# Attention and SoLU feed-forward on one core: q and k loaded in rows of eight tokens, and both turned by TensorE

## Chip, cores and metric

The kernel runs on one core of a Trainium2 chip. The metric is the device time of one execution in microseconds, from several executions; a time named "span" is the length of one profiled execution as the trace has it.

## What is computed

Four sequences of 768 tokens, eight heads of 64, go through an attention with a local window of 96 keys and eight global keys. The result, one row of 512 per token, goes through a feed-forward layer with the SoLU activation and a norm.

```python
batch, n_heads, seq, head_dim = (4, 8, 768, 64); n_global, n_local = (8, 96)
scores = scale * np.matmul(q, k.transpose(0, 1, 3, 2))
keep = is_global | is_local
scores = np.where(keep, scores + bias[None], -1e9)      # bias: -slope(head) * distance
a = softmax(scores); attn_out = np.matmul(a, v)
x = attn_out.transpose(0, 2, 1, 3).reshape(B * S, H * D)
h = x @ w_in                                            # 512 -> 1024
solu = h * softmax(h)
ln = (solu - mean) / sqrt(var + 1e-6) * g_ln
out = ln @ w_out                                        # 1024 -> 512, 3072 rows, float32
```

Inputs and output are float32; the kernel multiplies in fp16.

## The kernel before

**Units.** The work is cut into twelve units of 256 tokens (`UQ`), unit u being the stretch u mod 3 of sequence u div 3. A unit needs its own q, k and v (512 KB each) and, except the first of a sequence, the last keys of the unit before.

**Steps.** Every piece of work is a step with a short name, and the string `ORDER` (line 25) is the whole program: line 640 runs its steps in that order, each engine and each DMA queue gets its instructions in that order, and nothing is rearranged later. A letter after a step's name is the engine or queue (S SyncE, A ScalarE, P GpSimd, D VectorE), numbers are the unit and the head pair, half or token tile. The steps that matter here:

- `q`, `k`, `v` (lines 147 and 155): loads into a staging pool of 13 buffers (line 145). For q and k, a partition takes two neighbouring tokens of each of the eight heads, so a run in HBM is 512 bytes. v goes in two halves of 128 tokens, in runs of 256 bytes.
- `cq`, `ck`, `cv` (287, 291): casts to fp16, on any of three engines.
- `tk` and `tq` (295): eight 128x128 transposes on TensorE into one of two PSUM buffers with the tag "small" (line 128). `ek` (310) evacuates k and puts its tokens in order with a strided read; `eq` (306) evacuates q as it stands. Units 0, 1 and 2 turn q this way. The other nine units turn q with `dq` (315), a transpose done by the DMA queue from SBUF to SBUF.
- q therefore stays in an order of even tokens, then odd tokens, and so do the masks (`off`, 173), the scores `S` (328), the sums `L` (388), the weighted values `V` (418) and the normed result `N` (442). The store (551) writes rows "(p r)", two neighbouring tokens per partition, which this order fits.
- `X` (341) is the exponential of a head pair's scores on ScalarE, `M` (347) the multiplication with the mask on VectorE, `mask` (281) the sixteen mask tables on ScalarE, `I` (412) the reciprocal of the sums on ScalarE as two activations, `gk`, `gS`, `gX`, `gv0`, `gv` the eight global keys.
- The feed-forward of a token tile of 128: `A` (454, eight matmuls of 512 columns), `E` (468, exp on ScalarE), `U` (476, product on VectorE), `Q` (486, squares on ScalarE), `Z` (492, the norm's factors on GpSimd), `d` (527, DMA transpose of the product), `O` (531, eight matmuls of 512 columns), `o` (540, scaling out of PSUM), `st` (551, store).
- `wi` (559) loads w_in from GpSimd's queue with a cast; `warm` (226) issues matmuls on zeros whose result nobody reads.

PSUM: three double-bank buffers with the tag "big" (line 125), shared by `S`, `L`, `V` and `A`; two "small" ones, shared by turned tiles, `gS`, `gv`, `O` and `warm`. A step that asks for a buffer waits until the tile two (small) or three (big) allocations back has been read.

Of the kernel before, what the change touches and what calls it, by code (L numbers as in the profile page):

```python
# [18 lines left out]
UQ = 256  # L19
FAR = 30000.0  # L20
# [17 lines left out]
cq:P:5 k:S:5 ck:P:5 mean S:4:0 X:4:0 S:4:3 X:4:3 ce:0 ce:1 cq:D:6 ce:2 ce:3 ce:4 cm sm:5 sm:6 pr:7
v:S:6:0 q:S:7 A:2:0 gv:1 M:3:0 A:1:0 Q:0:0 E:2:0 U:2:0 Z:P:0:0 gk:2 E:1:0 U:1:0 A:1:1 v:S:4:0
E:1:1 U:1:1 L:3 I:3 tk:5 ek:D:5 sm:7 V:3 gS:4 Q:1:0 A:2:1 E:2:1 dq:S:5 N:3 S:5:0 X:5:0 M:4:3 A:3:0  # L40
E:3:0 S:5:3 gX:4 X:5:3 S:5:1 X:5:1 d:S:0:1 O:0:1 k:S:7 dq:S:6 d:S:0:0 S:5:2 X:5:2 gS:5 v:S:4:1
v:S:6:1 S:6:0 gX:5 X:6:0 U:2:1 Q:2:1 U:3:0 cq:D:7 dq:S:7 A:3:1 E:3:1 ck:D:7 S:6:3 cv:P:6 X:6:3
q:S:8 v:S:5:0 v:S:5:1 M:4:1 M:4:2 M:4:0 cv:P:4 gv0:2 Z:P:1:0 L:4 I:4 tk:7 O:0:0 S:6:1 X:6:1
o:A:0:0 M:5:0 o:D:0:1 cq:P:8 M:5:3 M:5:1 cv:P:5 U:3:1 M:5:2 ek:D:7 V:4 N:4 S:6:2 X:6:2 k:S:8 S:7:0
X:7:0 gv:2 gS:6 gX:6 v:S:7:0 v:S:7:1 S:7:1 X:7:1 S:7:3 X:7:3 L:5 I:5 M:6:3 M:6:0 V:5 N:5 A:4:0
E:4:0 ck:P:8 tk:8 ek:D:8 Q:2:0 Z:P:2:1 Z:P:2:0 Q:1:1 S:7:2 X:7:2 M:7:1 M:7:3 A:5:0 E:5:0 dq:S:8
U:4:0 d:S:1:0 O:1:0 d:S:2:0 M:6:2 o:D:1:0 U:5:0 k:S:9 d:S:1:1 S:8:2 X:8:2 Q:3:0 S:8:0 X:8:0
Z:P:1:1 ck:P:9 q:S:9 q:S:10 M:7:0 O:2:0 o:D:2:0 M:7:2 M:6:1 k:S:10 tk:9 S:8:1 X:8:1 ek:D:9 gk:3
cv:P:7 ck:P:10 A:4:1 E:4:1 L:6 U:4:1 k:S:11 d:S:2:1 cq:D:10 dq:S:10 I:6 S:8:3 X:8:3 d:S:3:1 O:1:1
o:D:1:1 d:S:3:0 V:6 cq:D:9 dq:S:9 Q:3:1 v:S:8:0 st:S:0 gS:8 gS:7 gX:7 v:S:8:1 v:S:9:0 v:S:9:1  # L50
d:S:4:0 A:5:1 d:S:5:0 gX:8 N:6 tk:10 Q:4:0 E:5:1 L:7 I:7 Z:P:3:1 Q:5:0 ck:D:11 A:6:0 tk:11 q:S:11
st:S:1 ek:D:10 M:8:1 U:5:1 d:S:5:1 d:S:4:1 M:8:0 ek:D:11 M:8:2 V:7 N:7 Q:4:1 S:10:0 E:6:0 gS:10
gX:10 X:10:0 O:2:1 o:A:2:1 O:3:1 U:6:0 M:8:3 Q:6:0 Z:P:3:0 Q:5:1 cv:P:8 S:10:3 S:9:3 X:9:3 M:9:3
X:10:3 Z:P:4:0 Z:P:5:1 st:S:2 A:6:1 E:6:1 U:6:1 Q:6:1 v:S:10:0 v:S:10:1 O:3:0 o:D:3:0 o:D:3:1
A:7:0 E:7:0 U:7:0 A:7:1 E:7:1 U:7:1 M:10:3 Z:P:5:0 cq:P:11 dq:S:11 O:4:0 o:D:4:0 Q:7:0 S:10:2
X:10:2 Q:7:1 V:8 L:8 I:8 N:8 M:10:0 S:10:1 cv:A:9 X:10:1 O:5:0 o:A:5:0 O:5:1 o:A:5:1 d:S:6:0
st:S:3 Z:P:7:0 Z:P:4:1 gv0:3 M:10:2 A:8:0 E:8:0 U:8:0 M:10:1 A:8:1 gv:3 E:8:1 U:8:1 O:4:1 S:11:1
X:11:1 Z:P:6:0 L:10 I:10 S:9:2 S:11:2 Z:P:6:1 Z:P:7:1 cv:P:10 o:D:4:1 X:11:2 O:6:0 X:9:2 d:S:6:1
O:6:1 d:S:8:0 st:S:5 S:9:1 X:9:1 st:S:4 S:9:0 X:9:0 Q:8:0 o:D:6:0 M:9:2 o:D:6:1 gS:9 M:9:0 d:S:7:1
v:S:11:0 d:S:7:0 Z:P:8:0 V:10 N:10 M:9:1 gX:9 S:11:3 S:11:0 X:11:0 O:8:0 X:11:3 M:11:1 gS:11 gX:11  # L60
L:9 o:A:8:0 I:9 V:9 N:9 st:S:6 d:S:8:1 M:11:0 A:10:0 E:10:0 Q:8:1 v:S:11:1 U:10:0 M:11:3 M:11:2
cv:P:11 A:10:1 E:10:1 A:9:0 U:10:1 E:9:0 U:9:0 Q:10:1 O:7:0 o:A:7:0 Q:9:0 L:11 I:11 V:11 N:11
Z:P:8:1 Q:10:0 A:9:1 Z:P:9:0 d:S:10:0 E:9:1 U:9:1 Z:P:10:1 O:7:1 o:A:7:1 A:11:0:0 d:S:9:0 O:8:1
o:A:8:1 Z:P:10:0 A:11:0:1 A:11:1:0 E:11:0:0 Q:9:1 O:10:0 E:11:0:1 o:A:10:0 U:11:0:0 E:11:1:0
Q:11:0:0 O:9:0 d:S:9:1 U:11:0:1 U:11:1:0 A:11:1:1 E:11:1:1 U:11:1:1 st:S:8 o:A:9:0 Z:P:9:1 O:9:1
o:A:9:1 d:S:10:1 O:10:1 o:A:10:1 Q:11:0:1 t:11:0:0 e:D:11:0:0 t:11:0:1 e:D:11:0:1 st:S:7 t:11:1:0
e:D:11:1:0 t:11:1:1 e:A:11:1:1 O:11:0:0 O:11:0:1 st:S:10 O:11:1:0 O:11:1:1 st:S:9 Z:P:11:0:1
o:D:11:0:0 o:D:11:0:1 st:S:11:0:1 Q:11:1:0 Q:11:1:1 Z:P:11:1:1 o:A:11:1:1 o:D:11:1:0 st:S:11:0:0
st:S:11:1:0 st:A:11:1:1
# [4 lines left out]
def kernel(  # L74
# [23 lines left out]
    QC = UQ // 2  # L98
    assert NL % 2 == 0 and NL < P and NG % 2 == 0 and 2 * NG <= 32 and H == 8
# [47 lines left out]
    def load_qk(queue, name, u):  # L147
        b, s = units[u]
        t = held[name + "32", u] = staged([P, H, 2 * D], name + "32")
        queues[queue].dma_start(  # L150
            out=t,
            in_=(q if name == "q" else k)[b, :, ts(s, UQ)].rearrange("h (p r) d -> p h (r d)", r=2),
        )
# [19 lines left out]
    def offsets(kind):  # L173

        w = (W0, W1)[kind]
        qi = held["qi", kind] = msb.tile([P, w], I32, name=f"qi{kind}", tag="osb", bufs=3)
        for j, a, e, o in blocks(kind)[0]:
            n = (e - a) // 2
            nc.gpsimd.iota(
                qi[:, o : o + 2 * n].rearrange("p (r i) -> p r i", r=2),  # L180
                pattern=[[1, 2], [2, n]], base=kind * UQ + a - j * P, channel_multiplier=-1,
            )
# [43 lines left out]
    def warm_up(n):  # L226

        t = small([P, 512], FP32, "warm")
        for _ in range(n):
            nc.tensor.matmul(out=t, lhsT=held["zeros"][:, 0:P], rhs=held["zeros"],  # L230
                             start=True, stop=True)
# [55 lines left out]
    def cast_qk(engine, name, u):  # L287
        t = held[name + "16", u] = attn.tile([P, 2, H, D], FP16, name=name + "16")
        cast(engine, t, held.pop((name + "32", u)).rearrange("p h (r d) -> p r h d", r=2))
# [5 lines left out]
    def turn(name, u):  # L295
        src = held.pop((name + "16", u))
        t = held["p" + name, u] = small([P, 2, NPAIR, P], FP16, name + "turned")
        for r in range(2):
            for g in range(NPAIR):
                nc.tensor.transpose(  # L300
                    out=t[:, r, g, :],
                    in_=src[:, r, 2 * g : 2 * g + 2].rearrange("p h d -> p (h d)"),
                    identity=held["ident"],
                )

    def evac_q(engine, u):
        t = held["qT", u] = attn.tile([P, 2, NPAIR, QC], FP16, name="qT")
        cast(engine, t, held.pop(("pq", u)))

    def evac_k(engine, u):  # L310
        t = held["kT", u] = attn.tile([P, NPAIR, UQ], FP16, name="kT", bufs=4)
        cast(engine, t.rearrange("p g (i r) -> p g i r", r=2),
             held.pop(("pk", u)).rearrange("p r g i -> p g i r"))

    def turn_q_dma(queue, u):
        t = held["qT", u] = attn.tile([P, 2, NPAIR, QC], FP16, name="qT")
        queues[queue].dma_start_transpose(
            out=t.rearrange("p r g i -> p (r g) i"),
            in_=held.pop(("q16", u)).rearrange("p r h d -> p (r h d)"),
        )  # L320
# [7 lines left out]
    def scores(u, g):  # L328
# [3 lines left out]
        for j, a, e, o in blocks(s)[0]:  # L332
            for m in range(2):
                r = slice(m * D, m * D + D)
                nc.tensor.matmul(  # L335
                    out=sc[:, m, o : o + e - a].rearrange("p (r i) -> p r i", r=2),
                    lhsT=held["kT", u - s + j // 2][r, g, ts(j % 2, P)],
                    rhs=qT[r, :, g, a // 2 : e // 2], start=True, stop=True,
                )
# [14 lines left out]
    def gstart(s):  # L354
        return 0 if s else G0 // 2

    def global_scores(u):
# [3 lines left out]
        n = QC - i0  # L361
        gs = held["gs", u] = small([P, 2, n], FP32, "gs")
# [314 lines left out]
```

## Time and profile before

| | |
|---|---|
| median of 5 executions | 182.15 us (181.33 to 185.22) |
| the profiled execution | 180.99 us, its span 179.3 us |
| mean TensorE clock granted | 0.965 |
| busy in the span: TensorE, ScalarE, VectorE, GpSimd | 149.3, 144.2, 113.1, 86.4 us |
| DMA: share of the 16 engines on SyncE's and ScalarE's loads and stores (queue q1) | 89.0% |
| q and k: 12 loads each of 512 KB, median time from issue to landing | 6.7 and 7.0 us |
| DMA transposes: 9 of q, 22 in the feed-forward | 4.9 and 3.7 us |

In the views, PE is TensorE, PEld its weight loads, DVE VectorE, ACT ScalarE, POOL GpSimd, SP SyncE. A letter q after an engine means its sequencer, which issues DMAs. Matmul rows contain their pipeline's depth, so the length of one row is no rate; the distance between the starts of rows is.

### The profile page before, as it was taken

What the parts mean: (1) busy time and instruction counts of PE and PEld (TensorE: products, weight loads), DVE (VectorE), ACT (ScalarE), POOL (GpSimd) and SP (SyncE); (2) the same over time, 40 slices, a digit from 0 to 9 for tenths busy, and PEclk for the clock granted to TensorE, in tenths of its full rate; (3) what the DMA queues carried; (4) which work ended last, traced back from release to release, by engine and by line L of the source; (5) the groups of instructions that cost most, each with busy time, mean ns of one, the idle gap of its engine ahead of it and who ended that gap; (6) DMA issues with size and microseconds to landing.
All of it is one profiled execution on the core that took longest, in us unless ns stands there. A gap on an engine that the chain in (4) does not pass through costs nothing. (4 is left out here: it accounts for less than half of the span.)

```text
span 179.3 us, 3846 instructions
## 1 busy us (share of the span) xinstructions
PE 149.3 (83%) x1456; PEld 79.9 (45%) x1456; DVE 113.1 (63%) x180; ACT 144.2 (80%) x232; POOL 86.4 (48%) x188
## 2 busy tenths in 40 slices
PE   0474538996699699799999999999999999998780
PEld 0353325634553444456445564455455545343430
DVE  6217357189697887995998993673566496314421
ACT  4498995859995989988988999699768988966541
POOL 6040280038159831988444822787881136732070
PEclk9999965799999999999999999999999999999997
DMA  5999999999999988999999999999969943067062
GB/s 118 277 290 251 271 227 168 268 327 246 202 299 249 201 107 167 221 250 153 207 292 236 142 227 260 183 256 264 279 132 278 225 89 59 18 155 240 27 235 88
DMA packets 87506, 36.69 MB, mean 205 GB/s; under 512 B 59456, under 2 KB 84544, under 8 KB 87488
## 3 DMA queue, kind: packets, MB, share of 16 engines
q1 hardware_dynamic: 83680, 34.74, 89.0%
q0 software_dynamic: 544, 1.05, 3.3%
q10 hardware_dynamic: 3264, 0.66, 2.4%
q8 instruction: 11, 0.18, 0.4%
q14 instruction: 7, 0.06, 0.1%
HBM read 23.07 MB, written 6.29 MB: 164 GB/s over the span
## 5 line engine op out<-in xcount | busy, mean ns | idle before, releaser
L344 ACT ACTIVATE pt<-sc 128x896 f16<-128x896 f32 (+1 forms) x48 | 40.0, 864 | 7.3 <-PE sc L335 6.8
L459 PE MATMUL ph<-w_in,xT 128*128 128x512 f16 x192 | 44.9, 380 | 0.7 <-DVE un L481 0.5
L535 PE MATMUL po<-gw,uT 128*128 128x512 f16 x192 | 44.6, 379 | 0.3 <-DVE osb L547 0.2
L481 DVE SCALAR_TENSOR_TENSOR un<-e,ph 128x1024 f16<-128x1024 f16 (+1 forms) x26 | 29.1, 1135 | 16.3 <-ACT e L473 7.6
L351 DVE TENSOR_TENSOR pt<-pt,mask 128x896 f16<-128x896 f16 (+1 forms) x48 | 30.6, 665 | 5.0 <-ACT pt L344 4.3
L473 ACT ACTIVATE e<-ph 128x1024 f16<-128x1024 f32 (+1 forms) x26 | 24.8, 955 | 5.5 <-PE ph L459 4.8
L535 PEld LDWEIGHTS <-uT 128*128 128x128 f16 x192 | 18.1, 98 | 22.1 <-issue 0.7
L490 ACT ACTIVATE sq<-un 128x1024 f16<-128x1024 f16 (+1 forms) x26 | 25.7, 988 | 2.7 <-DVE un L481 2.5
L459 PEld LDWEIGHTS <-xT 128*128 128x128 f16 x192 | 17.5, 98 | 23.1 <-issue 2.0
L444 DVE TENSOR_TENSOR xT<-pa,rlb 128x1024 f16<-128x1024 f32 x12 | 14.6, 1220 | 17.7 <-ACT rlb L416 16.3
L335 PE MATMUL sc<-qT,kT 64*128 64x128 f16 (+2 forms) x256 | 17.1, 251 | 5.7 <-ACT qT L135 2.5
L139 POOL CAST v<-v 128x1024 f16<-128x1024 f32 x9 | 9.9, 1110 | 19.8 <-DMA v<-in_v_dram 19.7
L510 POOL TENSOR_SCALAR w<-s,w 128x1 f32<-128x1 f32 x22 | 7.6, 344 | 17.1 <-ACT sq L490 11.3
L335 PEld LDWEIGHTS <-kT 64*128 64x128 f16 x256 | 9.3, 101 | 14.2 <-issue 10.3
L137 DVE COPY kT<-kturned 128x1024 f16<-128x1024 f16 x10 | 12.2, 1219 | 4.7 <-PE kturned L300 4.7
L398 PE MATMUL lb<-pt,ones 128*64 128x128 f16 (+2 forms) x256 | 11.5, 240 | 3.9 <-DVE un L481 3.1
L512 POOL TENSOR_TENSOR rs<-w,neghalf 128x1 f32<-128x1 f32 x24 | 13.7, 572 | 2.0
L549 ACT ACTIVATE osb<-po,rs 128x512 f32<-128x512 f32 (+1 forms) x13 | 8.6, 670 | 5.8 <-PE po L535 3.1
L416 ACT ACTIVATE rlb<-rlb 128x1024 f32<-128x1024 f32 x12 | 12.7, 1057 | 0.4
L547 DVE TENSOR_SCALAR osb<-po,rs 128x512 f32<-128x512 f32 (+1 forms) x13 | 8.7, 684 | 6.6 <-POOL both L501 2.3
L427 PE MATMUL pa<-pt,v 128*64 128x128 f16 (+2 forms) x256 | 11.7, 240 | 1.4 <-DVE v L137 1.4
L414 ACT ACTIVATE rlb<-lb 128x1024 f32<-128x1024 f32 x12 | 12.3, 1029 | 0.6 <-PE lb L406 0.6
(85 smaller groups left out, 185.3 us busy)
## 6 DMA issues: line engine op xcount, KB each, us to landing
q<-in_q_dram SPq DMA_DIRECT2D x12, 512.0 KB, 6.7
k<-in_k_dram SPq DMA_DIRECT2D x12, 512.0 KB, 7.0
v<-in_v_dram SPq DMA_DIRECT2D x22, 256.0 KB, 5.3
out_dram<-osb SPq DMA_DIRECT2D x11, 512.0 KB, 3.6
w_out<-in_moe_w_out_dram SPq DMA_DIRECT2D x4, 512.0 KB, 10.3
w_in<-in_moe_w_in_dram POOLq DMA_DIRECT2D x2, 512.0 KB, 8.4
v<-in_v_dram ACTq DMA_DIRECT2D x2, 256.0 KB, 6.3
out_dram<-osb SPq DMA_DIRECT2D x3, 128.0 KB, 1.9
```

What stands on the lines that cost most here:

```text
L335: nc.tensor.matmul(out=sc[:, m, o : o + e - a].rearrange("p (r i) -> p r i", r=2), lhsT=held["kT", u - s + j // 2][r, g, ts(j % 2, P)], rh ...
L344: nc.scalar.activation(out=pt[:, :, 0:w], in_=held.pop(("sc", u, g))[:, :, 0:w], func=AF.Exp, scale=inv_sqrt_d)
L351: nc.vector.tensor_tensor(out=pt[:, :, 0:w], in0=pt[:, :, 0:w], in1=held["mask"][:, g, :, o : o + w], op=ALU.mult)
L414: nc.scalar.activation(out=rlb, in_=held.pop(("lb", u)).rearrange("p g r i -> p g (r i)"), func=AF.Ln)
L416: nc.scalar.activation(out=rlb, in_=rlb, func=AF.Exp, scale=-1.0)
L444: nc.vector.tensor_tensor(out=xT, in0=held.pop(("pa", u)).rearrange("p g r i -> p g (r i)"), in1=held.pop(("rlb", u)), op=ALU.mult,)
L459: nc.tensor.matmul(out=held["ph", t][:, ts(fh, 512)], lhsT=held["xT", t[0]][:, j, ts(t[1], P)], rhs=held["w_in"][:, j, ts(fh, 512)], start ...
L473: nc.scalar.activation(out=held["e", t][:, f], in_=held["ph", t][:, f], func=AF.Exp, accum_out=s0)
L481: nc.vector.scalar_tensor_tensor(out=held["un", t][:, f], in0=held["e", t][:, f], scalar=1.0, in1=held["ph", t][:, f], op0=ALU.mult, op1=A ...
L490: nc.scalar.activation(out=sq[:, f], in_=held["un", t][:, f], func=AF.Square, accum_out=s2)
L512: eng.tensor_tensor(out=rs, in0=w3, in1=held["neghalf"], op=ALU.pow)
L535: nc.tensor.matmul(out=held["po", t], lhsT=held["uT", t][:, c, :], rhs=held["gw"][:, c, :], start=(c == 0), stop=(c == NFC - 1),)
```

## The change

q and k are loaded in rows of eight tokens: a partition takes eight neighbouring tokens of one head, a run of 2 KB. The partition is 4 x (token group) + (head pair), and the tile's halves m are the two heads of the pair. Each load becomes two of 256 KB, one per half, each with its own place and queue in the order. A transpose takes one token row r of both heads; its 128 columns are (token group, head pair), and the evacuation `eq` or `ek` reads PSUM with a stride so that the result is [pair, token] in token order. All twelve q are turned on TensorE; `dq` is gone. Masks, scores, sums and values are in token order, and `norm` reads with a stride of two elements to give the store its even-odd order. `ORDER` is another one throughout: 33 of the q and k halves are issued from SyncE, 12 from GpSimd and 3 from ScalarE; of v's halves 14, 9 and 1; six `warm` steps instead of one, four of them at the very end.

```diff
+NR = 8
...
-gb id off:1 cap off:0 g:A dist:1 mask:1:0 dist:0 q:S:0 cq:A:0 tq:0 eq:A:0 zero k:S:0 ck:D:0 tk:0
-ek:A:0 S:0:3 gk:0 mask:1:6 X:0:3 S:0:0 X:0:0 gS:0 mask:0:7 gX:0 v:A:0:0 mask:1:7 mask:0:2 mask:0:6
-q:S:1 cq:D:1 k:S:1 mask:0:5 mask:0:1 S:0:1 S:0:2 X:0:1 tq:1 eq:A:1 ck:P:1 selV tk:1 ek:D:1 S:1:0
-k:S:3 X:0:2 mask:0:3 ck:D:3 tk:3 q:S:2 v:S:0:1 ek:A:3 gk:1 fill cq:D:2 cv:D:0 gv0:0 q:S:4 q:S:3
-cq:D:3 S:1:3 mask:0:4 mask:1:2 v:S:2:0 X:1:0 mask:0:0 mask:1:3 mask:1:1 S:1:2 X:1:3 X:1:2 tq:2
-eq:A:2 M:0:1 M:0:0 S:1:1 hm k:S:2 gv:0 X:1:1 gS:1 ck:D:2 tk:2 M:1:0 ek:D:2 k:S:4 v:S:2:1 ck:A:4
-gX:1 gS:2 M:1:1 M:0:2 cq:P:4 S:2:3 X:2:3 M:0:3 S:2:1 X:2:1 tk:4 S:2:2 X:2:2 S:2:0 X:2:0 gX:2
-mask:1:5 L:0 I:0 M:2:3 V:0 warm:12 dq:S:3 S:3:1 X:3:1 N:0 M:2:0 M:1:3 mask:1:4 wi:0 wi:2 A:0:1
...
-E:1:1 U:1:1 L:3 I:3 tk:5 ek:D:5 sm:7 V:3 gS:4 Q:1:0 A:2:1 E:2:1 dq:S:5 N:3 S:5:0 X:5:0 M:4:3 A:3:0
...
+zero g:A id gb k:P:2:0 cap off:1 dist:1 fill k:P:2:1 off:0 dist:0 k:A:0:0 k:A:0:1 ck:D:0 q:S:0:0
+q:S:0:1 cq:P:0 tq:0 eq:D:0 hm q:S:1:0 k:S:3:0 q:S:1:1 q:S:2:0 k:S:1:0 k:S:3:1 v:S:0:0 q:S:2:1
+k:S:5:0 mask:1:7 k:A:1:1 mask:0:7 mask:0:0 mask:0:4 selV v:A:0:1 tk:0 cq:P:1 mask:0:1 mask:1:2
+mask:1:1 tq:1 mask:0:2 mask:0:5 ek:A:0 S:0:0 S:0:3 mask:0:6 ck:D:2 tk:2 ek:D:2 k:P:5:1 ck:P:1 tk:1
+ek:D:1 ck:P:3 S:0:1 gk:0 gS:0 eq:A:1 mask:1:3 gS:1 X:0:3 M:0:3 mask:0:3 mask:1:6 mask:1:0 S:0:2
+k:S:4:0 q:S:4:0 q:S:4:1 k:S:4:1 S:1:0 cv:P:0 gv0:0 cq:P:2 gX:0 q:S:5:0 q:P:5:1 X:0:0 q:P:3:0
+q:S:3:1 wi:0 ck:D:5 v:S:1:0 v:S:1:1 ck:P:4 k:P:6:0 k:S:6:1 v:S:2:0 wo:S:6 S:1:3 X:0:1 M:0:1 X:0:2
+M:0:2 X:1:0 gX:1 mask:1:4 gv:0 S:1:1 k:S:8:0 X:1:1 mask:1:5 tq:2 M:0:0 X:1:3 eq:D:2 tk:3 M:1:3
+ek:D:3 S:1:2 X:1:2 S:2:1 X:2:1 M:2:1 S:2:0 X:2:0 gS:2 gX:2 S:2:2 X:2:2 cq:P:4 M:1:2 M:1:1 M:1:0
+S:2:3 X:2:3 M:2:0 M:2:2 tk:4 ek:A:4 cq:P:3 gk:1 wi:2 v:P:2:1 v:S:3:0 wo:S:0 ck:P:6 v:P:3:1 L:0 I:0
+tq:4 eq:D:4 L:1 I:1 cq:D:5 tq:3 eq:D:3 k:S:8:1 wo:S:2 q:P:6:0 q:S:6:1 wo:S:4 warm:5:3 V:0 M:2:3
+N:0 cv:D:1 S:3:0 X:3:0 S:3:2 X:3:2 tk:5 ek:D:5 gS:4 gX:4 S:3:1 X:3:1 S:4:1 X:4:1 V:1 N:1 M:3:2
+q:S:7:0 q:S:7:1 v:S:4:0 v:S:4:1 M:4:1 k:S:7:0 S:3:3 X:3:3 M:3:3 S:4:0 gS:3 X:4:0 tk:6 ek:D:6 S:4:3
+X:4:3 gX:3 M:4:0 S:4:2 X:4:2 M:4:3 A:0:0 E:0:0 cv:A:2 A:1:0 E:1:0 A:1:1 M:3:1 U:0:0 M:4:2 Q:0:0
...
+st:S:8 e:D:11:1:1 E:9:1 U:9:1 d:S:10:1 d:S:9:1 O:10:0 O:11:1:0 O:11:1:1 Q:11:1:1 o:A:9:0 O:10:1
+Z:P:11:1:1 o:D:11:1:1 st:S:11:1:1 o:D:11:1:0 st:S:11:1:0 st:S:11:0:0 Q:9:1 o:A:10:0 Z:P:10:1
+o:A:10:1 st:S:10 O:9:1 Z:P:9:1 o:A:9:1 st:S:9 warm:4:4 warm:5:2 warm:4:5 warm:5:1
...
-    def load_qk(queue, name, u):
+    def load_qk(queue, name, u, m):
         b, s = units[u]
-        t = held[name + "32", u] = staged([P, H, 2 * D], name + "32")
-        queues[queue].dma_start(
-            out=t,
-            in_=(q if name == "q" else k)[b, :, ts(s, UQ)].rearrange("h (p r) d -> p h (r d)", r=2),
-        )
+
+        if (name + "32", u) not in held:
+            held[name + "32", u] = staged([P, 2, NR * D], name + "32")
+        src = (q if name == "q" else k)[b, :, ts(s, UQ)].rearrange(
+            "(g m) (i r) d -> m i g (r d)", m=2, r=NR)
+        queues[queue].dma_start(out=held[name + "32", u][:, m], in_=src[m])
...
-    def warm_up(n):
+    def warm_up(n, i=0):
...
-        t = held[name + "16", u] = attn.tile([P, 2, H, D], FP16, name=name + "16")
-        cast(engine, t, held.pop((name + "32", u)).rearrange("p h (r d) -> p r h d", r=2))
+        t = held[name + "16", u] = attn.tile([P, NR, 2, D], FP16, name=name + "16")
+        cast(engine, t, held.pop((name + "32", u)).rearrange("p m (r d) -> p r m d", r=NR))
...
     def turn(name, u):
         src = held.pop((name + "16", u))
-        t = held["p" + name, u] = small([P, 2, NPAIR, P], FP16, name + "turned")
-        for r in range(2):
-            for g in range(NPAIR):
-                nc.tensor.transpose(
-                    out=t[:, r, g, :],
-                    in_=src[:, r, 2 * g : 2 * g + 2].rearrange("p h d -> p (h d)"),
-                    identity=held["ident"],
-                )
-
-    def evac_q(engine, u):
-        t = held["qT", u] = attn.tile([P, 2, NPAIR, QC], FP16, name="qT")
-        cast(engine, t, held.pop(("pq", u)))
-
-    def evac_k(engine, u):
-        t = held["kT", u] = attn.tile([P, NPAIR, UQ], FP16, name="kT", bufs=4)
-        cast(engine, t.rearrange("p g (i r) -> p g i r", r=2),
-             held.pop(("pk", u)).rearrange("p r g i -> p g i r"))
-
-    def turn_q_dma(queue, u):
-        t = held["qT", u] = attn.tile([P, 2, NPAIR, QC], FP16, name="qT")
-        queues[queue].dma_start_transpose(
-            out=t.rearrange("p r g i -> p (r g) i"),
-            in_=held.pop(("q16", u)).rearrange("p r h d -> p (r h d)"),
-        )
+        t = held["p" + name, u] = small([P, NR, P], FP16, name + "turned")
+        for r in range(NR):
+            nc.tensor.transpose(out=t[:, r], in_=src[:, r].rearrange("p m d -> p (m d)"),
+                                identity=held["ident"])
+
+    def evac_qk(engine, name, u):
+
+        t = held[name + "T", u] = attn.tile([P, NPAIR, UQ], FP16, name=name + "T",
+                                            bufs=2 if name == "q" else 4)
+        cast(engine, t.rearrange("p g (i r) -> p g i r", r=NR),
+             held.pop(("p" + name, u)).rearrange("p r (i g) -> p g i r", g=NPAIR))
...
-                    out=sc[:, m, o : o + e - a].rearrange("p (r i) -> p r i", r=2),
+                    out=sc[:, m, o : o + e - a],
                     lhsT=held["kT", u - s + j // 2][r, g, ts(j % 2, P)],
-                    rhs=qT[r, :, g, a // 2 : e // 2], start=True, stop=True,
+                    rhs=qT[r, g, a:e], start=True, stop=True,
...
     def norm(u):
+
         xT = held["xT", u] = attn.tile([P, NPAIR, UQ], FP16, name="xT", bufs=3)
         nc.vector.tensor_tensor(
-            out=xT, in0=held.pop(("pa", u)).rearrange("p g r i -> p g (r i)"),
-            in1=held.pop(("rlb", u)), op=ALU.mult,
+            out=xT.rearrange("p g (r i) -> p g r i", r=2),
+            in0=held.pop(("pa", u)).rearrange("p g (i r) -> p g r i", r=2),
+            in1=held.pop(("rlb", u)).rearrange("p g (i r) -> p g r i", r=2), op=ALU.mult,
         )
...
-        "q": lambda e, u: load_qk(e, "q", u), "k": lambda e, u: load_qk(e, "k", u), "v": load_v,
+        "q": lambda e, u, m: load_qk(e, "q", u, m), "k": lambda e, u, m: load_qk(e, "k", u, m), "v": load_v,
...
-        "tq": lambda u: turn("q", u), "tk": lambda u: turn("k", u), "eq": evac_q, "ek": evac_k,
+        "tq": lambda u: turn("q", u), "tk": lambda u: turn("k", u), "eq": lambda e, u: evac_qk(e, "q", u), "ek": lambda e, u: evac_qk(e, "k", u),
-        "dq": turn_q_dma, "gX": global_expo, "gv0": global_v0, "gv": global_values, "L": sums, "I": invert,
+        "gX": global_expo, "gv0": global_v0, "gv": global_values, "L": sums, "I": invert,
```

The masks' offsets, the sums, the values and the global keys change as `scores` does: the even-odd views and the halved ranges go.

## Prediction

> **What bounds the kernel now.** I began with the page's busy lines and slices. TensorE is busiest, ScalarE next, and the DMA engines are full until about 143 us.
>
> ```profile
> PE 149.3 (83%) x1456; PEld 79.9 (45%) x1456; DVE 113.1 (63%) x180; ACT 144.2 (80%) x232; POOL 86.4 (48%) x188
> ...
> DMA  5999999999999988999999999999969943067062
> ```
>
> An average over stages says little, so next I read busy time by stage. Columns: window, PE, PEld, DVE, ACT, POOL, clock, DMA share, GB/s.
>
> ```profile
> 0.00:20.00 20.00, 9.04 (x86) 6.57 (x87) 8.45 (x22) 14.08 (x23) 5.70 (x25) 1.00 1.05 240
> 20.00:40.00 20.00, 14.48 (x129) 8.25 (x129) 11.50 (x19) 15.16 (x22) 5.56 (x7) 0.74 1.15 252
> 40.00:65.00 25.00, 20.19 (x260) 11.50 (x259) 21.20 (x31) 22.07 (x35) 16.34 (x25) 1.00 1.06 225
> 65.00:90.00 25.00, 23.58 (x268) 12.24 (x267) 21.36 (x30) 23.05 (x37) 14.89 (x25) 1.00 1.09 192
> 90.00:120.00 30.00, 29.57 (x283) 15.23 (x283) 23.57 (x35) 27.05 (x46) 16.12 (x35) 1.00 1.15 230
> 120.00:150.00 30.00, 30.00 (x305) 15.76 (x301) 18.76 (x30) 25.40 (x40) 16.50 (x38) 1.00 0.88 194
> ```
>
> Two regimes: until 65 us TensorE has gaps and ScalarE is the fuller engine (51.3 of 65 us busy, so 13.7 idle); after it TensorE is all but full. To check the second I priced TensorE's steps by the distance between starts in its timeline (columns: start, length):
>
> ```profile
> 61.17 0.62 PE L300 MATMUL kturned<-ident,k 128*128 128x128 f16 x8
> 61.72 0.80 PE L427 MATMUL pa<-pt,v 128*64 128x224 f16 x16
> 62.45 0.21 PE L437 MATMUL pa<-pg,vgz 64*128 64x32 f16 x4
> 62.59 0.29 PE L364 MATMUL gs<-qT,kgz 128*32 128x256 f16 x4
> 62.82 1.90 PE L459 MATMUL ph<-w_in,xT 128*128 128x512 f16 x8
> 64.65 0.37 PE L335 MATMUL sc<-qT,kT 64*128 64x96 f16 x6
> ```
>
> Eight transposes take 0.55 us, `A` or `O` 1.83, a pair's scores 0.30 (0.26 in a sequence's first unit), and by the same reading `L` or `V` 1.22 (0.88), `gS` 0.22 (0.13), `gv` 0.21, `mean` 1.82, a warm matmul 0.225. All steps make 145.1 us. Those ahead of `A:3:0`, which starts at 64.95, make 36.7; so 108.4 remain, to 173.4, and the last matmul ends at 174.28. Over 109 us TensorE loses about 1 us. From 65 us on TensorE is the bound; before it, ScalarE with its supply.
>
> **What the Trainium skill says.** Its page "DMA: Bandwidth & Descriptors", section "Why small descriptors are slow (HBM only)", gives each packet a fixed overhead. The trace agrees: a 512-byte packet takes 32 ns, a 2 KB one of w_out 91 (mean), so four short ones cost 1.4 times a long one. "TensorE: Matmul & The Clock Gate", "Part 4: PE-mode transpose", gives about 275 ns for one transpose in a kernel and adds a PSUM copy; rows here show 219 to 314 ns, but eight cost 0.55 us in a stream, and the trace decides. "SBUF — State Buffer", "SBUF: two separate sides", warns that a DMA issued from GpSimd gets its descriptors written by GpSimd, which VectorE can lock out: 620 ns alone, 3100 beside a copy. The trace before has only two such DMAs, at 846 ns of POOL each; it shows no lockout. The same page, under "Door 1: The DMA port swizzle", has two accesses to a 16-byte line at full speed, so the norm's float32 stride of two should be free; no run here shows it.
>
> **The change part by part.**
>
> *Loads.* q and k move in 24,576 packets of 512 bytes at 32.4 ns: 24,576 x 32.4 / 16 = 49.7 us of 16 engines. In 6,144 packets of 2 KB at 91 ns: 34.9. Minus 14.8 us. In the steady stage this hides: the trace shows waits for data mainly as these, on POOL, which is half idle.
>
> ```profile
> POOL v L139 <- DMA v<-in_v_dram: 19.7, 3, 7.0
> ...
> DVE q L137 <- DMA q<-in_q_dram: 4.1, 2, 3.0
> ...
> DVE k L137 <- DMA k<-in_k_dram: 2.2, 1, 2.2
> ```
>
> It can pay only in the first 40 us, where the casts wait 6.3 us on VectorE and 1 to 2 on ScalarE. Halving adds 24 issues at about 0.5 us of a queue; and in the changed program each load takes one of eight completion semaphores, so a load waits for the eighth before it: 2 MB in flight instead of 4. At 16 x 2048 bytes in 91 ns, 360 GB/s, that is still 5.8 us of work, as long as a landing; I take nothing for it.
>
> *`dq` goes.* Nine DMA transposes, 1,024 packets of 256 bytes at 25 ns: 9 x 1024 x 25 / 16 = 14.4 us of DMA, and on SyncE nine issues of 1.2 to 4.4 us with about 17 us of waits. What is queued behind them, loads and `d`, can go sooner. `d` lands in 3.7 us, `O` follows far later; hidden.
>
> *Turning on TensorE.* Nine turns more: 9 x 0.55 = 4.95 us, all behind or inside the full stage, so it counts in whole. Nine more evacuations: by the new order VectorE has 17 (10 before) at 1.22 us, +8.5, ScalarE 7 (5), +2.0 at 1.03; scaling moves the other way, ScalarE's `o` 13 to 11. VectorE is at 63% and ScalarE has 17 us to spare between 65 and 175 (92.4 busy); the direct cost is nothing. But each turned tile holds one of the two small buffers that `O` needs until VectorE, with its 1.22 us products, has read it. If an evacuation comes late by half such a product TensorE waits: 0 to 9 x 0.6 = 5.4 us; I take 1.5.
>
> *Strides.* The evacuation now steps 256 bytes in PSUM. The k evacuation of before steps 1 KB and takes ScalarE 1023 ns, the contiguous q 1033: nothing. The norm, 12 x 1.22 us: 0, or, half as long again, 7 us on VectorE, off the path.
>
> *POOL.* 21 loads are issued there. SyncE's take about 0.5 us when its queue has room, w_in's 0.85 here; at 0.6 us, 13 us more; if v's 1,024 runs cost in proportion (four times w_in's 256), 3.4 us for each of nine. Bounds +13 and +38 us on an engine with 93 us free, but its casts of q and k feed TensorE early.
>
> *Warm matmuls.* 17 instead of 12 before the last `O`: +1.1 us. The 18 at the end cost 18 x 0.225 = 4.1 us, and wait for the last scaling, beside a store of 3.0 to 3.6 us plus about 1.1 to the end: hidden, at worst 0.5.
>
> *The start.* New total up to the last `O`: 145.1 + 4.95 + 1.1 = 151.2. Ahead of `A:4:0` stand 45.75 (24 + 2 pairs of scores, 17 turns, five `L` and `V`, six `A`), so 105.4 remain. With the same 1 us loss the end is equal if `A:4:0` starts at 174.28 - 106.4 = 67.9. What ScalarE must have done by then: 16 masks 7.1, 24 exponentials 18.6, `gX` 1.8, four evacuations 3.7, five `I` at 2.04, six `E` at 1.0, three `Q`, `cv`, `sc`, `cm` 6.4: 53.8 us. Its idle decides. The new order gives POOL two load issues before the offsets that the masks need, so I put the first mask at about 5.3 us (3.76 before), 2 more lost for the second distance table, 1.3 for the second q (its cast stands on POOL behind `hm`, which waits for VectorE), then a full stage, as all first loads have landed by about 11 us instead of 20; and 2.9, as between 40 and 65 before: 11.5, so 65.3. TensorE itself needs 27.0 us from `A:0:0`, whose buffer `X:4:0` must have read: 29 us of ScalarE's list, 8.6 idle, 1 for hand-offs, so 38.7 and with it 65.7. With idle as before (13.7): 67.5. I take 67.0, a gain of 0.9.
>
> *Sum.* 67.0 + 105.4 + 1.0 + 1.5 = 174.9 to the last matmul, 0.6 later than before. The end: 0.7 scaling and 3.0 to 3.6 + 1.1 for a 512 KB store, taken as 5.2, where 5.0 was: +0.2. Span 180.1, the execution 180.99 + 0.8 = 181.8; the median stands 1.16 above that execution, so **182.9 us**, which is no change: I take about 0.5% as what a measurement here tells from none.
>
> **Rivals.**
>
> *The start gains in full.* The first loads stop starving ScalarE, `A:4:0` starts at 64, buffers don't bind. For it: 13.7 us idle before 65. Against: the masks start later, and TensorE needs 27 us from `A:0:0`. 64 + 105.4 + 1 + 5.0 + 1.7 + 1.2 = **178.3**.
>
> *POOL is late*, and the kernel slower. The nine v issues from GpSimd take 3.4 us or are locked out by VectorE, and the casts of q and k (16 of 24 are now on POOL) queue behind them, so turns, and with them TensorE, wait. Against: POOL's idle. It decides once an issue takes over about 3 us: `A:4:0` at 71, and 2 us later on: 71 + 105.4 + 1 + 1.5 + 2 + 5.2 + 2.9 = **189.0**.
>
> **How the numbers follow.** No change 0.42 (own range 181.0 to 184.8), full gain 0.30, late POOL 0.28. Below 181.2, faster by over 0.5%: 0.05 + 0.285 = 0.335; above 183.1: 0.195 + 0.28 = 0.475; between, 0.19. The range goes from the gain's 178.3 less a little, 178.0, to 188.0, just short of POOL's full price; it covers the bounds of the buffers' cost.
>
> **What would show it.** Right: in the changed profile `A:4:0` (the seventh group of eight on `ff_in`'s line) starts near 67, TensorE is full after it, DMA is at three quarters instead of full, turned tiles stay at 0.55 us. The full gain shows by that group near 64; late POOL by POOL over 110 us busy and `kturned` or `qturned` waiting for POOL's casts. Wrong would be a TensorE with gaps after 67 us that wait for evacuations or `uT`, or a stretch of strided reads longer than 1.22 us.

## The result, and the profile after

The changed kernel takes 179.75 us (median of 31 executions, 177.81 to 182.01), the kernel before 183.17 (58 executions on the same chips). The ratio is 0.988, 95% interval 0.986 to 0.991: **1.2% faster**. The kernel before falls into two groups, 29 executions from 180.31 to 182.82 us and 29 from 183.52 to 186.76, and since ratios leave out executions more than 1.5% above the fastest of their kernel, thus that second group, they aren't quotients of medians (0.981 here). 0.01 of ratio is 1.8 us. The profiled execution has a span of 176.7 us (before 179.3).

From the page after, the rows of busy time and slices, and the queues of the loads and stores, q1 of SyncE and ScalarE (89.0% before) and q0 of GpSimd (3.3% before):

```profile
PE 155.7 (88%) x1551; PEld 85.2 (48%) x1551; DVE 123.9 (70%) x185; ACT 143.7 (81%) x231; POOL 107.1 (61%) x214
...
DMA  4999999999999998089999850339991593137553
...
q1 hardware_dynamic: 45648, 26.35, 63.3%
q0 software_dynamic: 2224, 6.56, 14.9%
```

TensorE works 6.4 us more in a span 2.6 us shorter, VectorE 10.8 more, GpSimd 20.7 more, ScalarE the same. A part of what left q1 went to q0: together they take 138.2 us of the 16 engines, before 165.5. The same stages as before (window, PE, PEld, DVE, ACT, POOL, clock, DMA share, GB/s):

```profile
0.00:20.00 20.00, 7.12 (x70) 5.17 (x71) 10.52 (x24) 11.45 (x22) 12.77 (x32) 1.00 0.94 303
20.00:40.00 20.00, 17.78 (x262) 11.62 (x257) 19.47 (x26) 19.81 (x29) 12.56 (x16) 1.00 1.11 301
40.00:65.00 25.00, 21.24 (x209) 11.53 (x208) 22.29 (x28) 21.25 (x32) 17.22 (x25) 1.00 1.08 212
65.00:90.00 25.00, 24.84 (x285) 13.89 (x285) 23.04 (x34) 23.77 (x38) 18.85 (x30) 1.00 0.86 178
90.00:120.00 30.00, 30.00 (x309) 15.97 (x306) 21.64 (x30) 28.20 (x45) 20.43 (x44) 1.00 0.66 131
120.00:150.00 30.00, 30.00 (x310) 15.82 (x308) 17.97 (x30) 24.20 (x39) 12.80 (x30) 1.00 0.74 164
```

The first 20 us are worse (PE 9.04 before, ACT 14.08), the next 20 better (14.48 and 15.16 before), and after 65 us TensorE is full. DMA sinks there to between 0.66 and 0.86 (0.88 to 1.15 before). The granted clock is 1.00 from 65 to 150 us in both, so the late stage doesn't differ by it. What TensorE waits for between 65 and 176 us, first before, then after (total us, times, longest):

```profile
PE lT L518 <- DVE uT L137: 1.1, 2, 0.6
PE lb L398 <- DVE pt L351: 0.8, 1, 0.8
PE ph L459 <- DVE un L481: 0.5, 1, 0.5
PE kturned L300 <- POOL k L139: 0.3, 1, 0.3
PE sc L335 <- DVE kT L137: 0.3, 1, 0.3
PE ph L459 <- DVE xT L444: 0.2, 1, 0.2
PE po L535 <- DVE osb L547: 0.2, 1, 0.2
```

```profile
PE warm L231 <- ACT osb L536: 1.0, 1, 1.0
```

Seven causes with 3.4 us before; after, one, and that is a warm matmul at the very end. None of the seven is for a turned q or a load: six are for VectorE, one for a cast on GpSimd. VectorE's work from 65 to 150 us is nearly the same, 63.7 us before and 62.7 after; what differs is when it is done.

Each wait costs more than the idle time shown, since a row's length holds the pipeline's depth. Before, at one of them:

```profile
159.91 3.62 PE L535 MATMUL po<-gw,uT 128*128 128x512 f16 x16
163.99 1.02 PE L459 MATMUL ph<-w_in,xT 128*128 128x512 f16 x4 [0.47 <-DVE un L481]
```

From 159.91 to 163.99 are 4.08 us; sixteen such matmuls take 3.46 without a wait (next view), so this one cost 0.62 us where 0.47 is shown. By the same reckoning the seven cost about 4.6 us. TensorE's rows after, in a part with feed-forward groups back to back (start, length):

```profile
143.34 1.90 PE L446 MATMUL ph<-w_in,xT 128*128 128x512 f16 x8
145.08 1.89 PE L522 MATMUL po<-gw,uT 128*128 128x512 f16 x8
146.80 3.62 PE L446 MATMUL ph<-w_in,xT 128*128 128x512 f16 x16
150.26 3.62 PE L522 MATMUL po<-gw,uT 128*128 128x512 f16 x16
153.71 0.61 PE L505 MATMUL lT<-ident,un 128*128 128x128 f16 x8
```

Sixteen matmuls from start to start take 3.46 us, eight take 1.73. The prediction's 1.83 came from one group with scores behind it (62.82 to 64.65), so it holds 0.1 us of that hand-over: from `A:4:0` on, 28 of the 42 groups of `A` and `O` stand before another such group, a transpose or a warm matmul and take 1.73 (two of them up to 0.26 more), and 14 stand before scores, sums, values or global keys and take 1.82. TensorE's end after:

```profile
161.77 8.99 PE L522 MATMUL po<-gw,uT 128*128 128x512 f16 x40
170.60 1.03 PE L231 MATMUL warm<-zeros 128*128 128x512 f16 x4
172.63 3.18 PE L231 MATMUL warm<-zeros 128*128 128x512 f16 x14 [1.01 <-ACT osb L536]
```

The last `O` ends at 170.8 (161.77 + 8.99), against 174.28 before. `A:4:0` starts at 69.66, later than forecast; so the gain lies behind it, in the **late block**: from the start of `A:4:0` to the end of the last `O`. It takes 101.1 us; the prediction held it for 105.4 + 1.0 + 1.5.

### The profile page after: what moved, and what is told of

It reads as the page before. It is cut to its first block, busy times and chain, and to the rows that moved or that the text cites. A ratio compares the mean times of both kernels' runs of the same rounds, so it can differ in the third digit from the quotient of the medians.

```text
span 176.7 us, 4095 instructions
## 1 busy us (share of the span) xinstructions
PE 155.7 (88%) x1551; PEld 85.2 (48%) x1551; DVE 123.9 (70%) x185; ACT 143.7 (81%) x231; POOL 107.1 (61%) x214
## 5 line engine op out<-in xcount | busy, mean ns | idle before, releaser
L339 DVE TENSOR_TENSOR pt<-pt,mask 128x896 f16<-128x896 f16 (+1 forms) x48 | 28.9, 637 | 7.9 <-ACT pt L332 7.9
L446 PEld LDWEIGHTS <-xT 128*128 128x128 f16 x192 | 18.1, 98 | 22.6 <-issue 2.0
L300 PE MATMUL qturned<-ident,q 128*128 128x128 f16 x96 | 8.6, 242 | 14.7 <-POOL q L142 11.4
L323 PE MATMUL sc<-qT,kT 64*128 64x128 f16 (+2 forms) x256 | 15.8, 248 | 0.8 <-ACT pt L332 0.4
L430 DVE TENSOR_TENSOR xT<-pa,rlb 128x1024 f16<-128x1024 f32 x12 | 14.6, 1220 | 2.3 <-ACT rlb L402 1.7
L300 PEld LDWEIGHTS <-q 128*128 128x128 f16 x96 | 6.8, 108 | 17.0 <-POOL q L142 12.9
L140 DVE COPY kT<-kturned 128x1024 f16<-128x1024 f16 x9 | 10.8, 1215 | 5.6 <-PE kturned L300 5.6
L534 DVE TENSOR_SCALAR osb<-po,rs 128x512 f32<-128x512 f32 (+1 forms) x15 | 10.6, 713 | 5.4 <-POOL rs L499 2.7
L492 POOL TENSOR_SCALAR w<-s 128x1 f32<-128x1 f32 x22 | 7.9, 360 | 8.8 <-ACT e L460 6.7
L142 POOL CAST k<-k 128x1024 f16<-128x1024 f32 x8 | 9.2, 1155 | 6.1 <-PE kturned L300 5.4
L142 POOL CAST q<-q 128x1024 f16<-128x1024 f32 x8 | 9.4, 1178 | 5.1 <-issue 2.6
```

The lines of the kernel that those rows point to most:

```text
L142: nc.gpsimd.tensor_copy(out=out, in_=in_)
L300: nc.tensor.transpose(out=t[:, r], in_=src[:, r].rearrange("p m d -> p (m d)"), identity=held["ident"])
L323: nc.tensor.matmul(out=sc[:, m, o : o + e - a], lhsT=held["kT", u - s + j // 2][r, g, ts(j % 2, P)], rhs=qT[r, g, a:e], start=True, stop=True,
L339: nc.vector.tensor_tensor(out=pt[:, :, 0:w], in0=pt[:, :, 0:w], in1=held["mask"][:, g, :, o : o + w], op=ALU.mult)
L430: nc.vector.tensor_tensor(out=xT.rearrange("p g (r i) -> p g r i", r=2), in0=held.pop(("pa", u)).rearrange("p g (i r) -> p g r i", r=2), i ...
L446: nc.tensor.matmul(out=held["ph", t][:, ts(fh, 512)], lhsT=held["xT", t[0]][:, j, ts(t[1], P)], rhs=held["w_in"][:, j, ts(fh, 512)], start ...
```

## The experiments

Theory A: before, TensorE lost about 5 us after 65 us to waits in its order, and the new order, not the layout, takes them away. Theory B: the longer runs do it, by an earlier start. Every interval is 95%, every ratio to the kernel before; a figure "over the changed kernel" comes from the difference of two such ratios.

### Is TensorE the bound, and what does a turn cost there?

**Late turns four times.**

```diff
 for r in range(NR):
-    nc.tensor.transpose(...)
+    for _ in range(4 if name == "q" and u > 7 else 1):
+        nc.tensor.transpose(...)
```

> The changed kernel with the TensorE turning of q done four times for the four units 8 to 11 only, all of whose turns start after the feed-forward group of unit 4 (69.7 us): 96 transposes more that write the same values again. In the kernel that turned twice the second turning lengthened a group by 0.45 us. Theory A (from there on TensorE never waits, so each instruction counts in whole): 4 x 3 x 0.45 = +5.4 us, about 185, ratio to before 1.018. Theory B (turns also hide in the late stage): under +2 us, ratio under 1.00.

Measured: 184.34 us, ratio 1.020 (1.014 to 1.027), 5.8 us over the changed kernel. Its late block is 106.2 us (69.08 to 175.28). A turn of 32 shows the price:

```profile
87.96 1.96 PE L301 MATMUL qturned<-ident,q 128*128 128x128 f16 x32
89.75 0.61 PE L301 MATMUL kturned<-ident,k 128*128 128x128 f16 x8
90.29 0.97 PE L386 MATMUL lb<-pt,ones 128*64 128x96 f16 x24
```

32 transposes take 1.79 us to the next start, 56 ns each; eight before sums take 0.54, with the hand-over in it. In the late block TensorE's work counts in whole; theory A of this run holds.

**Early turns four times:** the same edit with `2 < u < 8`.

> The changed kernel with the TensorE turning of q done four times for the five units 3 to 7 only, all of whose turns start before the feed-forward group of unit 4: 120 transposes more, 5 x 3 x 0.45 = 6.75 us of TensorE. Theory A (before 69.7 us TensorE is idle for some 24 us in waits for loads and casts, and the turns fill them): under +2 us, ratio to before under 1.00. Theory B (the turns count in whole, as the prediction had it for all nine): +6.75 us, ratio near 1.025.

Measured: 181.92 us, ratio 1.001 (0.997 to 1.004): 2.2 us more for 6.75 us of work, with 0.7 us of uncertainty either way. Between the two theories, near A: about two thirds lie in TensorE's gaps. The profile agrees: the late block starts 2.1 us later, at 71.77, and takes 101.7.

**All nine turned twice:** the same edit with `2 if ... u > 2`.

> The changed kernel with the TensorE turning of q done twice for the nine units 3 to 11 (the second transposes write the same values again): 72 transposes more, which change nothing in the output. Theory A (TensorE is the bound of the changed kernel from 66 us, so each instruction on it counts in whole, as the prediction had it for the nine turns): 9 x 0.55 = +5.0 us on the changed kernel's 179.8, thus about 184.7, ratio to before near 1.01. Theory B (some turns lie in TensorE's gaps before 66 us, or behind waits for the vector engines): +2 to +3.5 us. If the turns were as good as free, the result would stay within 1 us of the changed kernel.

Measured: 178.98 us, ratio 0.987 (0.982 to 0.993), no slower than the changed kernel. Neither theory. By the two runs above it should cost 4 x 0.45 + a third of 5 x 0.45 = 2.5 us. Its late block is 102.6 us, 1.5 longer, nearly as priced; but it starts at 68.23, earlier than in any other profile of the changed kernel and its variants in the changed layout (69.1 to 71.8). What gave that back is a wait for VectorE ahead of a turn of q, first in the changed kernel (two rows of VectorE, one of TensorE), then in this run:

```profile
52.77 2.27 DVE L140 CAST q<-q 128x1024 f16<-128x1024 f32 x1
54.95 2.34 DVE L568 TENSOR_SCALAR gw<-w_out,g 128x512 f16<-128x512 f32 x1
...
57.94 0.61 PE L300 MATMUL qturned<-ident,q 128*128 128x128 f16 x8 [2.39 <-DVE vgz L372]
```

```profile
55.96 1.05 PE L301 MATMUL qturned<-ident,q 128*128 128x128 f16 x16 [0.29 <-DVE vgz L373]
```

`vgz`, a product on VectorE, has to read the small PSUM buffer that the turn takes next, and stands behind a cast of q and a scaling of w_out. In this run these took 1.09 and 1.42 us, so TensorE waited 0.29 instead of 2.39, and for w_in 0.18 instead of 1.33. The 3.3 us less of waits outweigh the 2.3 us of five early turns. So the run doesn't show turns to be free; why the cast and the scaling were shorter isn't shown (more in the last section).

### The order or the layout?

**New order, old layout:** the changed `ORDER`, all q turned by TensorE, but runs of 512 bytes and the even-odd order of tokens; each load is halved by heads.

```diff
-src = ....rearrange("(g m) (i r) d -> m i g (r d)", m=2, r=NR)
-dma_start(out=held[name + "32", u][:, m], in_=src[m])
+hs = slice(4 * m, 4 * m + 4)
+dma_start(out=held[name + "32", u][:, hs],
+          in_=...[b, hs, ts(s, UQ)].rearrange("h (p r) d -> p h (r d)", r=2))
```

> The new order and all twelve q turned on TensorE, but q and k still in rows of two tokens (512-byte runs, half of the heads per load) and the even-odd order throughout. Theory A (the order makes the gain, the runs only relieve a DMA that nobody waits for): within 1 us of the changed kernel, so about 1% faster than before. Theory B (2 KB runs make the order possible: the first loads land in time only with them): slower than the changed kernel by 3 us or more, so no faster than before; the casts of the first 40 us wait for loads and the first feed-forward matmuls start after 41 us instead of 38.7.

Measured: 180.11 us, ratio 0.996 (0.993 to 0.998). Its stages after 65 us:

```profile
65.00:90.00 25.00, 25.00 (x235) 12.61 (x234) 22.34 (x32) 23.58 (x39) 20.67 (x33) 1.00 0.96 166
90.00:120.00 30.00, 30.00 (x325) 16.79 (x324) 21.80 (x33) 28.14 (x45) 19.84 (x40) 1.00 0.72 154
120.00:150.00 30.00, 30.00 (x339) 16.19 (x338) 18.45 (x28) 23.94 (x36) 12.15 (x28) 1.00 0.72 162
```

TensorE never stops, and the late block is 101.0 us (72.87 to 164.97 + 8.85): the dense late stage comes with the order and the turning in it, without the layout. But the block starts 3.2 us later than in the changed kernel (one profile each), and the casts of k wait 3.3 us on VectorE for their loads, there 0.8; TensorE's third turn of q starts 2.2 us later (24.17, there 21.98). The rest of the 3.2 isn't clearly the layout's: this profile had a granted clock of 0.74 from 20 to 40 us and 0.93 from 40 to 65, the changed kernel's 1.00. The times don't hang on that: the 13 executions of this run at a mean clock of 0.99 or more have a median of 180.0 us, the nine of the changed kernel at 1.00 one of 178.4. So A for the late stage, B for the start: 0.4% came with the order and the turning, the other 0.7% with the layout; that the long runs at the start make it is what the waits for k speak for, but the runs weren't parted from the rest of the layout in this order.

**Long runs alone:** the kernel before with two loads of 256 KB where one of 512 KB stood.

```diff
+for m in range(2):
+    queues[queue].dma_start(out=t[:, 4*m : 4*m+4].rearrange("p h c -> p (h c)"), in_=src[m])
```

> The kernel before with q and k read in 2 KB runs, two loads of 256 KB at the place of each, and nothing else changed; the tokens then stand in the wrong places, so that the attention is computed on a wrong arrangement of q and k. Theory A (runs don't matter by themselves): within 1 us of before, with the DMA share down by about 15 us of 16 engines. Theory B (loads start the kernel): faster by 2 us or more, the first score exponentials earlier than 10.8 us and fewer waits of casts for loads.

Measured: 187.25 us, ratio 1.030 (1.023 to 1.036). Neither theory: the loads cost time. SyncE's issues at the start of the profiled execution, the longest of its six:

```profile
4.70 2.65 SPq L153 DMA_DIRECT2D k<-in_k_dram  x4
8.08 7.58 SPq L153 DMA_DIRECT2D q<-in_q_dram  x2
15.70 0.60 SPq L160 DMA_DIRECT2D v<-in_v_dram  x1
```

And what that queue waited for from 8 to 16 us:

```profile
SPq L153 <- DMA v<-in_v_dram: 6.5, 1, 6.5
```

A load of q waits 6.5 us for a load of v to land. The two share a completion semaphore: by the trace's semaphore events the loads of SyncE and ScalarE take eight of them in turn, and this q waits for the one that a load of v on ScalarE holds, issued at 12.04 and landed at 15.11 (the q goes out at 15.12). The DMA share of the first 20 us falls to 0.67 (1.05 before). How much of the 3.0% is due to such waits wasn't parted from the rest.

**Second halves issued by GpSimd:** the same with `"P" if m else queue`.

> The kernel before with q and k in 2 KB runs as in the run that did only this, but the second 256 KB half of each load issued by POOL (tokens stand in wrong places, as there). Theory A (runs alone lost 3.0% because twice as many loads shared SP's eight completion semaphores, so that half as many bytes were in flight; a second queue has semaphores of its own): the loss goes, ratio 0.99 to 1.00. Theory B (POOL pays some 0.6 us for each of 24 issues between its casts, masks and v loads, or is late with them): still 1 to 3% slower, with POOL waits before the casts.

Measured: 214.17 us, ratio 1.177 (1.167 to 1.186), far beyond both. GpSimd's issues:

```profile
4.47 0.55 POOL L153 DMA_DIRECT2D k<-in_k_dram  x1
13.99 0.47 POOL L327 COPY kgz<-kT 64x32 f16<-64x32 f16 x2 [8.96 <-ACT kT L135]
14.49 0.54 POOL L153 DMA_DIRECT2D q<-in_q_dram  x1
```

They cost 0.55 us each but stand behind a copy that waits 9 us for an evacuation, so GpSimd's third load goes out at 14.5 us. The run tells nothing of semaphores; it tells that loads on a computing engine are as late as the work ahead of them.

### Turning off the DMA queue in the old order

**All q on TensorE:** each `dq:S:u` becomes `tq:u eq:D:u`; four buffers for the turned q, and two evacuations moved ahead of a turn.

> The kernel before with its nine DMA transposes of q replaced, where they stand, by eight TensorE transposes and an evacuation on VectorE (four buffers for the turned q instead of two, two steps moved ahead). Theory 1 (TensorE is the bound from 65 us, as predicted): slower by 3 to 6 us, nine times 0.55 plus late evacuations. Theory 2 (TensorE's waits after 65 us, 3.4 us in the trace, absorb it): within 1.5 us of before.

Measured: 200.43 us, ratio 1.103 (1.096 to 1.110), 18.7 us: far above both.

```profile
65.00:90.00 25.00, 18.36 (x153) 9.19 (x152) 13.99 (x22) 13.13 (x21) 13.85 (x20) 0.80 0.57 107
90.00:120.00 30.00, 26.21 (x275) 14.15 (x270) 20.06 (x29) 21.04 (x33) 10.84 (x22) 0.89 0.51 119
```

All engines run dry at once and the granted clock falls to 0.80. Against the kernel before, TensorE idles 8.6 us more in these 55 us, the lower clock is worth up to 25 x 0.20 + 30 x 0.11 = 8.3 us, nine turns are 5.0. These are bounds that overlap, and more than the 18.7 measured.

**Only the last four units:** `tq:u eq:D:u` for u = 8 to 11.

> The kernel before with q of the four units 8 to 11 alone turned by TensorE and evacuated by VectorE at the places of its DMA transposes (four buffers for the turned q instead of two). All nine turned so cost 10.3%, 18.7 us. Theory A (an order of work that was written for a turning off the engines makes TensorE and VectorE wait in their queues for each cast and evacuation, about 2 us a unit): 4 x 2.1 = +8 us, ratio near 1.045. Theory B (only the work counts: 4 x 0.55 on TensorE): +2.2 us, ratio 1.012. Theory C (the loss sits in the five units before 90 us, where all engines run dry): within 1 us of TensorE's work, and the early units make the rest.

Measured: 190.28 us, ratio 1.050 (1.043 to 1.057), 9.1 us: theory A, 2.3 us a unit. One turn shows how (TensorE's rows):

```profile
98.91 0.21 PE L406 MATMUL lb<-pg,hm 64*128 64x32 f16 x4
101.97 0.62 PE L300 MATMUL qturned<-ident,q 128*128 128x128 f16 x8 [2.84 <-DVE q L137]
102.52 0.37 PE L335 MATMUL sc<-qT,kT 64*128 64x96 f16 x6
```

The turn takes 0.55 us and waits 2.84 for a cast that stands close before it in the order. That was harmless while a DMA queue did the waiting.

**q not turned, a VectorE copy instead.**

```diff
-queues[queue].dma_start_transpose(out=..., in_=...)
+nc.vector.tensor_copy(out=..., in_=...)
```

> The kernel before with the nine DMA transposes of q replaced by a plain VectorE copy of the unturned tile (it leaves the turning out of nine units). The DMA engines lose 14.4 us of work, VectorE gains nine copies of some 0.3 us. Theory A (the nine DMA transposes are hidden and the late stage is bound by TensorE and its waits for the vector engines): within 1 us of the kernel before. Theory B (the late gain of the change comes from taking the transposes off the DMA engines, which are full until 143 us): 2 to 4 us faster, with fewer waits of TensorE after 65 us.

Measured: 187.65 us, ratio 1.035 (1.030 to 1.040): slower, against both theories, though the DMA share between 90 and 120 us sinks from 1.15 to 0.63. The copies wait 2.5 us in VectorE's queue until TensorE has read an older turned q, and TensorE gains waits for what stands behind them, among these after 65 us (the profiled execution is the run's fastest, at 184.73, so it shows the lesser part of the loss):

```profile
PE gs L364 <- DVE osb L547: 1.2, 1, 1.2
...
PE sc L335 <- DVE un L481: 1.0, 1, 1.0
```

A step moved from a DMA queue into an engine's queue at the same place cost 6.4 us net here, even without TensorE. What the relief of the DMA engines is worth by itself can't be read from this run; it didn't outweigh the waits.

### Parts of the change

**No loads on GpSimd:** q, k and v issued by SyncE at the same places.

> The changed kernel with every q, k and v load of POOL's queue moved to SP's queue at the same place of the order. Theory A (POOL's issues cost 0.55 to 0.97 us each beside its casts, some 13 us of POOL's time, none of it on the path after 66 us): a gain or loss under 1 us. Theory B (a second queue with completion semaphores of its own keeps more loads in flight; on SP alone each load waits for the eighth before it, as in the kernel with runs only, which lost 3.0%): 2 to 5 us slower, with load issues on SP of several us each before 66 us.

Measured: 183.26 us, ratio 1.008 (1.004 to 1.012), 3.6 us over the changed kernel. The size is theory B's, the place isn't: `A:4:0` starts at 69.82. SyncE's rows:

```profile
122.71 8.19 SPq L516 DMA_TRANSPOSE uT<-un  x3
130.95 0.58 SPq L163 DMA_DIRECT2D v<-in_v_dram  x1
```

And TensorE's:

```profile
132.46 0.23 PE L412 MATMUL pa<-pt,v 128*64 128x96 f16 x2
135.45 0.93 PE L412 MATMUL pa<-pt,v 128*64 128x224 f16 x22 [2.76 <-ACT v L138]
...
137.03 3.55 PE L522 MATMUL po<-gw,uT 128*128 128x512 f16 x8 [0.20 <-ACT osb L536]
```

A load of v that GpSimd issues at 122.28 in the changed kernel stands here behind three transposes of `d`, goes out at 130.95 and stops TensorE for 2.76 us. Behind the stop the granted clock is 0.57 (137 to 141 us), and an `O` has 3.55 us instead of 1.89. Together these are 4.4 of the 4.7 us by which the late block is longer here.

**No warm steps at the end:** the last four `warm` steps deleted.

> The changed kernel without the four warm steps at its end (18 matmuls on zeros). As predicted (hidden beside the last store): no change within 0.5 us. Rival (the warm matmuls end last, as the chain of the changed kernel has it): the span is shorter by 0.3 to 1 us.

Measured: 179.25 us, ratio 0.988 (0.984 to 0.991): they are hidden.

**w_in early,** without the end's warm steps: `wi:2` next to `wi:0`.

> The changed kernel with the second w_in load issued next to the first, ten loads earlier, and without the four warm steps at the end. In the changed kernel the first feed-forward group waits 1.3 us for that load. Theory A (TensorE's queue at 38 to 66 us is filled by what its own order allows; a wait of 1.3 us there moves all that follows): about 1 us faster than the changed kernel, 178.5. Theory B (what ends the waits at 38 to 66 us is the q, k and v loads and the casts on POOL, and the w_in load only takes their place in the queue): no change or 1 us slower.

Measured: 178.58 us, ratio 0.983 (0.977 to 0.988). The wait for w_in is gone, but the late block starts at 71.23, no earlier. Ahead of `A:0:0`, which starts at 40.24 (38.69 in the changed kernel), TensorE now waits 1.6 us for casts of q and k on GpSimd, as theory B has it. But between 60 and 65 us this profile's granted clock is 0.73 (there 1.00), and `mean`, matmuls for the norm, takes 3.42 us instead of 1.89; so the run doesn't settle which theory holds. It is the fastest version by its middle; its interval overlaps the changed kernel's, so no gain is shown.

## Why the prediction was wrong

It forecast no change; the kernel is 1.2% faster.

- **The step that failed: "Over 109 us TensorE loses about 1 us", carried on as "the same 1 us loss".** The late block was priced at 105.4 us; done without a wait it takes 101.1. Of those 4.3 us, 2.4 are in the 42 groups of `A` and `O`, priced at 1.83 each and together 74.4 us long; the other 1.9 are in the small steps (scores 0.9, sums and values 0.6, turns 0.4), of which scores and turns, too, were priced with a hand-over behind them. The kernel before had, by the same prices, 108.4 - 105.4 = 3.0 us more to do behind `A:3:0`: 104.1 us, done in 109.3. It lost **5.2 us, not 1**; the seven waits above are 3.4 of it as idle time and about 4.6 from start to start. An overpriced list had hidden a loss that a new order could win back. The new order, tried with the old layout, has none of it. Which of its moves removes which wait wasn't tried.
- **"If an evacuation comes late ...; I take 1.5"**: 0 in the late block, where no wait of TensorE is for a small buffer. The one wait of this kind came earlier, 2.4 us for the buffer that `vgz` had to read, and is part of the start.
- **Nine turns, "so it counts in whole"**: right for the four behind `A:4:0`, 2.2 us; of the other five about a third counts, an estimate of 0.9 from the early-turns run. The prediction's 4.95 is so about 1.8 too much. The doubled run cost less than even this, for the reason given there.
- **The start**: `A:0:0` at 38.69 (38.7 forecast), but `A:4:0` at 69.66 instead of 67.0, 2.7 us worse: from `A:0:0` on, the forecast's 27.0 us of TensorE took 31.0, with waits of 1.3 us for w_in and 2.4 us for VectorE's `vgz` ahead of a turn. That 38.7 was met is partly luck: in the run without warm steps at the end, which has the same program up to there, `A:0:0` starts at 39.64.
- **"I take nothing" for the halved loads**: wrong on one queue, where they lost 3.0% together with the long runs. In the new order, with three queues, both layouts have halved loads, so no run prices the halving there. GpSimd's loads take eight completion semaphores of their own in the changed kernel, which the prediction's "one of eight" left out.
- **The end**: 5.9 us for 5.2.

The sum: 2.7 - 4.3 - 1.0 - 1.5 = -4.1 us to the last matmul (170.8 for 174.9), +0.7 behind it, 176.7 for 180.1.

Right were the hidden end, the strides and the DMA's relief (27.3 us of 16 engines, 14.8 + 14.4 = 29.2 forecast). Evacuations take 1215 and 1217 ns on VectorE (1219 before) and the norm 1220 as before. So for the norm's operand in SBUF the trace bears out what the Trainium skill ("SBUF — State Buffer", "Door 1: The DMA port swizzle") let expect of a stride of two; its other operand lies in PSUM, of which the prediction's citation doesn't speak, and cost nothing more either. That the transposes of q were hidden before fits the seven waits, none of which is for one. Of the rivals, "POOL is late" had its price refuted: a v issue took 971 ns, not 3.4 us. The full gain of the start didn't come either; 178.3 lies nearer to the time than the forecast, for another reason.

## What to carry to other kernels

Before you call an engine full, price its work from rows that stand back to back, not from one with a hand-over behind it, and list its waits in that stage: prices read so were 4.3 us too high here, and hid all but 1 of 5.2 us of loss. When a step moves from a DMA queue to an engine, price its place and not only its work: a turn cost 2.3 us a unit in an order written for the DMA queue, and 0.45 to 0.55 in one written for turns on TensorE. And a load is as late as the work ahead of it in its queue.

## What was not expected of the hardware

- Casts on VectorE took longer in the changed kernel at the same shape: q 1079 ns on average (762 before), v 1158 (686). In the two traces the ten casts with nothing beside them on GpSimd took 0.63 to 0.69 us, and the seven that took 0.79 us or more, up to 2.27, all ran beside a cast, a copy, a scaling or a load issue on GpSimd; some beside short GpSimd work kept to 0.69. This is a coincidence in time that no run varied, but it reaches TensorE: the 2.39 us ahead of the turn above are such a cast and such a scaling.
- The granted clock dropped in stretches of some executions. Of the changed kernel's 31, the nine at a mean clock of 1.00 took 177.81 to 178.83 us, the other 22, at 0.96 to 0.99, 179.50 or more; the profiled one, 178.43, is of the nine. In single profiles the clock between 20 and 40 us was 0.74 before, 1.00 after and 0.83 in the kernel turning twice. No run shows what sets it off.
